# One more buffer for finished output blocks, one fewer for exps, in an attention and GeGLU kernel

## The chip, the cores and the metric

The kernel runs on one core of a Trainium2 chip. The metric is device time in microseconds. Times quoted are medians of several executions.

## The reference

Two steps follow each other: an attention with a sliding window over 8 batches of 8 heads (half of the heads plain, half with every fourth position), then a GeGLU block over all 4608 tokens.

```python
scores = scale * q @ k.T;  scores = where(mask, scores, -1e9)
attn = exp(scores - max); attn = attn / sum(attn);  x = attn @ v     # (4608, 512)
g = x @ w_gate;  val = x @ w_val
out = (gelu(g) * val) @ w_out                                        # (4608, 512) float32
```

## The kernel before

The tokens are worked through in 9 chunks of 512. Each chunk has a gate part (the matmuls with `w_gate` and `w_val`, line 808) and an output part (the matmuls with `w_out`, line 842). The attention of the batches that later chunks need is woven in between: scores on TensorE, their exponentials on ScalarE (the exps, line 693), then the masking, a product with the mask on VectorE (line 698). TensorE sums up in accumulator banks; an eviction is the copy of a finished bank into an output block in SBUF, the on-chip memory (line 853). The parts that matter here, cut:

```python
prb = ctx.enter_context(tc.tile_pool(name="prb", bufs=7))     # exps
osbp = ctx.enter_context(tc.tile_pool(name="osbp", bufs=3))   # finished output blocks
# ...
def two_p_of(n):                       # exp of head pair n
    pt = prb.tile([P, LP], F16, tag="P", name=f"P{n}")
    nc.scalar.activation(pt[:, 0 : src.shape[1]], src, AF.Exp, bias=0.0, scale=scale)
# ...
def store(c, tb, bank, eng):           # block tb of chunk c: empty the bank, send it away
    osb = osbp.tile([P, DM], F32, tag="osb")
    if eng == "act":
        nc.scalar.activation(osb, ps[:, bank, :], AF.Copy, bias=0.0, scale=1.0 / USCALE)   # line 853
    # ...
    nc.sync.dma_start(out=out[t0 : t0 + P, :], in_=osb)                                    # line 857
```

The order of the program is the order by hand. A word like `e3@2` in it means "store block 3 of chunk 2", a number means "so many matmuls", and `R` stands for `load_rest(3)`, `load_first(4)`, `load_rest(4)`, that is, for the loads of two batches, all of them issued from SyncE (`nc.sync`):

```python
gates = {
    2: "G 6 e3@1 R 2 g0 3 u0 ...",     # chunk 2, gate part: the last store of chunk 1, then R
    3: "G 6 e3@2 2 g0 3 u0 2 g1 ...",  # chunk 3, gate part: the last store of chunk 2
}
```

So the fourth store of a chunk runs at the start of the next chunk, and the stores of chunk 2 stand behind `R` in SyncE's queue.

The softmax here doesn't subtract the row's maximum and nothing guards it: scores larger than these inputs give would overflow.

## Time and profile before

| | |
|---|---|
| time | 353.54 us (3 runs, 351.2 to 355.06) when the prediction was made |
| the profiled execution | 357.36 us, span 355.2 us |
| TensorE busy | 336.1 us, 95% of the span |
| VectorE, ScalarE, GpSimd | 175.6, 148.4 and 131.8 us |
| mean granted TensorE clock | 0.986 |

TensorE is the bound nearly everywhere.

### The profile page before, as it was taken

Reading aid. Unit: us, or ns where it says so; the run is one execution under the profiler, and the core shown is the slowest. Engines: PE = TensorE matmul, PEld = TensorE weight load, DVE = VectorE, ACT = ScalarE, POOL = GpSimd, SP = SyncE. Lnnn points to the kernel's source line nnn. Section 1 sums busy time; section 2 is a strip of 40 time slices with the busy share of each in tenths; the row PEclk is TensorE's granted clock in tenths of the full one; section 3 lists DMA queues with packets and bytes.
Section 4 is the critical chain, followed back from the end, with each engine's and each line's share of the span. In section 5 each row is a group of like instructions: output and inputs, shape, how many; then the busy total and the mean of one; then the engine's idle time right before and its main releaser. Section 6 shows DMA issues by size and latency. Waiting matters only on the chain.

```text
span 355.2 us, 5961 instructions
## 1 busy us (share of the span) xinstructions
PE 336.1 (95%) x2264; PEld 168.3 (47%) x2264; DVE 175.6 (49%) x276; ACT 148.4 (42%) x219; POOL 131.8 (37%) x193
## 2 busy tenths in 40 slices
PE   8889999599999999399999999999999999999996
PEld 3644454244554455144555456445654444444443
DVE  3786687244354444134598349744983204403320
ACT  2753372243683367134543357335533243322321
POOL 8892414498503738836604660376000000000000
PEclk9999999699999999899999999999999999999999
DMA  8999997998219779899449943894100020011002
GB/s 179 221 203 218 201 199 169 277 210 193 89 56 191 180 196 186 220 225 189 155 111 215 179 120 103 219 203 128 62 30 2 30 89 2 1 67 53 0 30 89
DMA packets 107804, 48.74 MB, mean 137 GB/s; under 512 B 84481, under 2 KB 103297, under 8 KB 107777
## 3 DMA queue, kind: packets, MB, share of 16 engines
q1 hardware_dynamic: 98208, 41.24, 50.2%
q0 software_dynamic: 9024, 6.43, 11.9%
q10 hardware_dynamic: 544, 0.72, 0.8%
q8 instruction: 17, 0.28, 0.3%
q14 instruction: 11, 0.08, 0.1%
HBM read 38.27 MB, written 9.44 MB: 134 GB/s over the span
## 4 chain that ended last, share of the span: by engine, by line
PE 65%; DMA 15%; SPq 9%; POOL 4%; DVE 4%; issue 2%; ACT 0%; POOLq 0%; DVEq 0%; ACTq 0%
PE ps L808 41%; PE ps L842 18%; DMA wo<-in_moe_w_out_dram 6%; PE ps L752 3%; DMA stage<-in_v_dram 3%; SPq L286 3%; DMA dense<-s 2%; DMA out_dram<-osb 2%; SPq L220 2%; PE ps L678 2%; SPq L289 2%; SPq L323 1%; DMA stage<-in_q_dram 1%; POOL q L346 1%; DVE xT L800 1%
## 5 line engine op out<-in xcount | busy, mean ns | idle before, releaser
L808 PE MATMUL ps<-xT,wv 128*128 128x512 f16 x432 | 115.8, 385 | 9.3 <-ACT osb L853 9.3
L1022 DVE SCALAR_TENSOR_TENSOR u_all<-g,ps 128x512 f16<-128x512 f16 x96 | 65.9, 686 | 112.8 <-PE ps L808 94.5
L808 PE MATMUL ps<-xT,wg 128*128 128x512 f16 x432 | 116.3, 384 | 1.0 <-POOL xT L934 0.7
L1017 ACT ACTIVATE g<-ps 128x512 f16<-128x512 f32 x96 | 57.2, 597 | 109.1 <-PE ps L808 109.1
L842 PE MATMUL ps<-wo,u_all 128*128 128x512 f16 x420 | 101.1, 379 | 0.1
L808 PEld LDWEIGHTS <-wv 128*128 128x128 f16 x432 | 42.5, 99 | 58.6 <-issue 10.5
L808 PEld LDWEIGHTS <-wg 128*128 128x128 f16 x432 | 42.4, 99 | 54.7 <-issue 7.2
L842 PEld LDWEIGHTS <-u_all 128*128 128x128 f16 x420 | 37.8, 98 | 38.7 <-issue 0.7
L346 POOL COPY q<-dense 64x512 f16<-64x512 f16 (+2 forms) x48 | 30.8, 670 | 28.8 <-DMA dense<-s 27.0
L853 ACT ACTIVATE osb<-ps 128x512 f32<-128x512 f32 x34 | 20.2, 595 | 45.5 <-PE ps L842 28.1
L292 POOL CAST s<-stage 128x1280 f16<-128x1280 f32 x12 | 15.0, 1251 | 47.0 <-DMA stage<-in_q_dram 34.0
L335 POOL CAST v<-stage 64x1152 f16<-64x1152 f32 x24 | 27.6, 1151 | 2.9 <-DMA stage<-in_v_dram 2.0
L693 ACT ACTIVATE P<-ps 128x768 f16<-128x768 f32 (+1 forms) x24 | 20.0, 835 | 18.1 <-PE ps L678 18.0
L800 DVE TENSOR_TENSOR xT<-ps,rb 128x576 f16<-128x576 f32 x24 | 22.4, 932 | 6.0 <-PE ps L752 3.2
L304 POOL CAST s<-stage 128x512 f16<-128x512 f32 x24 | 14.6, 637 | 12.8 <-DMA stage<-in_q_dram 11.1
L770 DVE STREAM_TRANSPOSE dt<-ps 128x576 f32<-128x576 f32 x17 | 13.1, 771 | 10.1 <-PE ps L752 10.1
L752 PEld LDWEIGHTS <-v 128*128 128x128 f16 x240 | 12.3, 98 | 5.6
L830 ACT ACTIVATE g<-ps 128x512 f16<-128x512 f32 x12 | 7.1, 597 | 14.7 <-PE ps L808 14.7
L787 DVE STREAM_TRANSPOSE rb<-rc 128x576 f32<-128x576 f32 x17 | 13.1, 769 | 0.1
L752 PEld LDWEIGHTS <-two_ones 128*128 128x128 f16 x132 | 10.4, 98 | 5.4 <-issue 0.3
L752 PE MATMUL ps<-P,v 128*128 128x96 f16 (+3 forms) x240 | 12.6, 199 | 0.0
L678 PEld LDWEIGHTS <-q 128*128 128x128 f16 x216 | 10.9, 98 | 3.3
(99 smaller groups left out, 231.0 us busy)
## 6 DMA issues: line engine op xcount, KB each, us to landing
out_dram<-osb SPq DMA_DIRECT2D x35, 256.0 KB, 2.1
stage<-in_v_dram SPq DMA_DIRECT2D x34, 128.0 KB, 3.3
stage<-in_v_dram SPq DMA_DIRECT2D x24, 144.0 KB, 4.0
stage<-in_q_dram SPq DMA_DIRECT2D x24, 128.0 KB, 3.2
stage<-in_k_dram SPq DMA_DIRECT2D x24, 128.0 KB, 2.9
stage<-in_q_dram SPq DMA_DIRECT2D x6, 512.0 KB, 4.8
stage<-in_k_dram SPq DMA_DIRECT2D x6, 512.0 KB, 5.7
wo<-in_moe_w_out_dram POOLq DMA_DIRECT2D x3, 512.0 KB, 20.6
```

The lines of the kernel that those rows point to most:

```text
L292: nc.gpsimd.tensor_copy(s16[:, 1280 * t : 1280 * t + 1280].rearrange("p (g k c) -> p k g c", g=2, k=5), st_of(i).rearrange("p (k g c) -> p ...
L335: nc.gpsimd.tensor_copy(dst[half, :, half], st[half])
L346: eng.tensor_copy(dst[half, :, :, half], src[half])
L678: nc.tensor.matmul(psf[:, base + c0 : base + c0 + w], lhs, rhs, start=True, stop=True, skip_group_check=True)
L693: nc.scalar.activation(pt[:, 0 : src.shape[1]], src, AF.Exp, bias=0.0, scale=scale)
L752: nc.tensor.matmul(o, lhs, rhs, start=st, stop=True, skip_group_check=True)
L800: nc.vector.tensor_tensor(dst, num, rb, ALU.mult)
L808: nc.tensor.matmul(ps[:, bank, :], w[:, kc, ns], xT[kc][:, tok], start=first, stop=end)
L842: nc.tensor.matmul(ps[:, bank, :], u_all[:, fc, tb * P : (tb + 1) * P], wo_t[fc // 4][:, fc % 4, :], start=(fc == 0), stop=(fc == NNB - 1),)
L853: nc.scalar.activation(osb, ps[:, bank, :], AF.Copy, bias=0.0, scale=1.0 / USCALE)
L1017: nc.scalar.activation(g, ps[:, gate_banks(c, args[0])[0], :], AF.Gelu)
L1022: nc.vector.scalar_tensor_tensor(u_all[:, nb, :], tiles.pop(("g", nb)), USCALE, val, ALU.mult, ALU.mult)
```

## The change

SBUF is nearly full. A fourth output block (2048 bytes per partition) is wanted so that a block can be filled while older ones still wait for their store, and a buffer for exps (1664 bytes) is given up to make room. Four blocks and seven exps do not fit: the build stops with 8 KB wanted for the blocks and 7.25 KB left.

```diff
-    prb = ctx.enter_context(tc.tile_pool(name="prb", bufs=7))
+    prb = ctx.enter_context(tc.tile_pool(name="prb", bufs=6))
     nrm = ctx.enter_context(tc.tile_pool(name="nrm", bufs=2))
     ffn = ctx.enter_context(tc.tile_pool(name="ffn", bufs=3))
-    osbp = ctx.enter_context(tc.tile_pool(name="osbp", bufs=3))
+    osbp = ctx.enter_context(tc.tile_pool(name="osbp", bufs=4))
```

The instructions on every engine are the same, in the same order.

## The prediction

> **What bounds the kernel now.** I read four views of the kernel before, in this order: the slices of the span, the list of waits, the chain of work that ended last, and the timeline and windows around two places. The slices first (a digit is the busy share of a slice of 8.9 us in tenths; PEclk is the granted TensorE clock in tenths):
>
> ```profile
> PE   8889999599999999399999999999999999999996
> PEclk9999999699999999899999999999999999999999
> ```
>
> TensorE is at 90% or more nearly everywhere after the start, so the kernel is bound by TensorE, except in slices 7 (62 to 71 us, digit 5, clock 6) and 16 (142 to 151 us, digit 3, clock 8). The list of waits (engine and line, what it waited for, us in total, times, longest) says what TensorE waited for there:
>
> ```profile
> ACT osb L853 <- DMA out_dram<-osb: 14.1, 2, 7.2
> PE ps L808 <- ACT osb L853: 9.3, 2, 5.7
> ```
>
> TensorE waited twice, 9.3 us in all, for ScalarE to empty an accumulator bank into an output block (osb). ScalarE itself waited twice, 14.1 us, for the DMA that carries an older output block away: the three blocks were all taken. The other waits of TensorE in that list sum to about 5.5 us, and most lie before 62 us. The timeline, cut to the lines concerned, shows where the DMA came late:
>
> ```profile
> 60.04 0.93 SPq L857 DMA_DIRECT2D out_dram<-osb  x2
> 66.12 0.60 ACT L853 ACTIVATE osb<-ps 128x512 f32<-128x512 f32 x1 [6.87 <-DMA out_dram<-osb]
> 66.77 0.58 PE L808 MATMUL ps<-xT,wv 128*128 128x512 f16 x1 [3.61 <-ACT osb L853]
> ...
> 145.27 1.51 SPq L857 DMA_DIRECT2D out_dram<-osb  x3
> 147.63 0.60 ACT L853 ACTIVATE osb<-ps 128x512 f32<-128x512 f32 x1 [7.22 <-DMA out_dram<-osb]
> 148.28 1.86 PE L808 MATMUL ps<-xT,wv 128*128 128x512 f16 x4 [5.70 <-ACT osb L853]
> ```
>
> The stores are short, but SyncE issues everything in program order. The first store of chunk 0 was ready at 54.2 us (its eviction started at 53.65 and took 0.59) and was issued at 60.04, behind the loads of batch 2. The first store of chunk 2 was ready at 128.8 and issued at 145.27, behind the loads of batches 3 and 4. Each time the fourth block of the same chunk needed exactly that first one's buffer. Its bank is the one that the next chunk's fourth group of matmuls writes, so TensorE stopped.
>
> The stop costs more than its idle time:
>
> ```profile
> 62.20:71.00 8.80, 5.19 (x24) 1.83 (x19) 2.13 (x2) 2.08 (x3) 3.71 (x6) 0.70 1.08 277
> 71.00:142.10 71.10, 71.10 (x483) 36.36 (x482) 31.26 (x46) 37.67 (x55) 40.90 (x64) 0.99 0.75 163
> 142.10:151.00 8.90, 3.20 (x10) 1.11 (x8) 1.37 (x2) 1.57 (x3) 7.22 (x11) 0.81 0.81 220
> ```
>
> These are windows: stretch, length, TensorE busy, weight loads, VectorE, ScalarE, GpSimd, granted clock, DMA share, GB/s. Between the two stops TensorE is busy 71.10 of 71.10 us at clock 0.99. Around them the clock is 0.70 and 0.81: the matmuls after a stop start every 0.43 us instead of every 0.216 us.
>
> **What the Trainium skill says.** "TensorE: Matmul & The Clock Gate", section "What's actually happening": the clock of the array halves after an idle window of about 3.4 us and comes back after about as long a busy time. The trace agrees in kind: stops of 3.61 and 5.70 us, then half rate for 5.8 us and 3.1 us. "DMA: Bandwidth & Descriptors", section "Anatomy of one DMA", says that a wait on a semaphore happens on the issuing sequencer before dispatch. That fits a ready store standing behind a waiting load on SyncE for 16.5 us. "SBUF — State Buffer", section "SBUF: two separate sides", says that a VectorE operation with two SBUF inputs and a GpSimd operation that reads SBUF exclude each other for a whole instruction. The trace agrees: the masking of the exps usually takes 0.49 to 0.59 us, but 1.14, 1.07 and 1.40 us in the three cases that fall on a GpSimd cast. "Perfetto Trace Analysis", section "Optimization Strategy", reads consistent bubbles as a sign of too few buffers. Here there are two lone ones, and the list of waits names the buffer.
>
> **The change part by part.** No instruction is added or removed; only waits move.
>
> Fourth output block. There are 36 output blocks in 9 chunks of 4. With three buffers, block i waits for the store of block i-3; with four, for that of i-4, the same block of the chunk before. Chunk 0 then has no such wait at all. Its fourth eviction can start when its bank is complete, about 61.7 us, and ends at 62.3; the matmul that needs the bank is due at 63.0. The fourth block of chunk 2 needs the store of chunk 1's fourth block, which ScalarE finished at 106.0 and SyncE sent at once, 34 us before it is wanted. Every later block has its older store away in time; the tightest is chunk 3's fourth (wanted at 183 us before, its partner sent at 172 us; after the change about 2 us of slack by my shift below). So both stops go:
> - First stop, idle: starts of matmuls at 62.78 and 66.77 are 3.99 apart instead of 0.22: 3.77 us.
> - First stop, slow clock: 17 matmuls from 66.77 to 73.27 took 6.50 us instead of 17 x 0.216 = 3.67: 2.83 us.
> - Second stop, idle: a group of four started at 141.55, the next matmul at 148.28: 6.73 - 0.86 = 5.87 us.
> - Second stop, slow clock: 8 matmuls from 148.28 to 151.36 took 3.08 instead of 1.73: 1.35 us.
> - Sum: 13.8 us. From 151 us to the end TensorE is busy 200.5 of 204 us (the rest is the tail), so what is won there is kept if the inputs arrive in time.
>
> Six exps instead of seven. Exp n then waits for the last matmul that reads exp n-6. The program makes exps of one chunk in a row and uses nearly all up before the next chunk's. The nearest pair is batch 6's third exp (217.14 us) and the matmuls of batch 5's first (186.99 us): 30 us apart. In the list of waits the exps wait only for their scores, 18.0 us in 19 times, never for a buffer. Cost: 0.
>
> What comes nearer. TensorE gains 6.6 us on the loads of batch 2 and 7.2 us more on those of batches 4 and 5, because SyncE and GpSimd do not get faster there. By the timeline: batch 2's dilated mask is complete on GpSimd at 85.3 us; the first masking ran at 92.86 and moves to 86.3, so 1 us is left. Batch 5's keys are spread at 166.4 us; its first scores ran at 177.7 and move to 170.5 on the same scale, so 4 us are left. Batch 4's values are ready at 149.6, first used after 169: 12 us left. None becomes a wait, if narrowly.
>
> A cost does come. GpSimd's work on batch 5 (164 to 175 us) slides 7.2 us into the stretch from 173 to 190 us, where the chain of work runs through VectorE with hardly any slack. There three or four maskings now fall on GpSimd work. At 0.25 us for the short copies and 0.6 us for the casts (from the excess of 0.55 to 0.9 us of the slowed ones), that is 1.1 us, and about 0.2 us more in chunk 1. I take 1.3 us off: 13.8 - 1.3 = 12.5 us.
>
> **The rivals.**
> 1. The store wait is only replaced: another wait of the same chunk start (gelu table, x of the next batch, mask) holds TensorE. For it: 1 us of slack at batch 2's mask. Against it: the start of chunk 2 (104 us) has the same program and no late store, and TensorE runs through it. If half the gain went, 347 us.
> 2. Loads become the bound after the second stop: SyncE's queue is busy without a break from 107 to 172 us, and the DMA share is near 0.8. If batch 5 came 5 us late, the time would be about 346 us.
> 3. The clock drop is chance: the stop of 3.61 us is barely long enough for it, so unprofiled runs may not always have had it. The runs before spread from 351.2 to 355.06, and the profiled one took 357.36. If the profile overstates the stops by 3.8 us, the gain is 8.7 us and the time 345 us.
> 4. Six exps bite: against it, 30 us of room. It would need a wait of 12 us to cancel the gain.
>
> **Range and chances.** 353.5 - 12.5 = 341.0 us. Everything going through with no collision gives 339.7 us, and the fastest run before suggests 2 us of spread, so the low end is 337.5; rivals 2 and 3 give the high end, 346. Faster by over 2% means under 346.5 us: 0.88. Within 2%: 0.11. Slower by over 2%: 0.01, since nothing is added that works.
>
> **What would show it.** In the profile after, slices 7 and 16 of TensorE should be 9, the clock should nowhere fall below 0.9 after the start, and neither line of the second fence should remain. ScalarE's exps should still wait for scores only. In the stretch after the second stop some maskings should take about 1.1 us, and TensorE should have a few tenths of idle more there. I am wrong if a new wait of several us stands at 63 or 136 us, if scores wait for a load of batch 2 or 5, or if a clock drop stays without a stop before it.

## The result, and the profile after

| | before | after |
|---|---|---|
| first comparison, median | 353.27 us (4 runs) | 342.88 us (4 runs, 342.2 to 343.35) |
| ratio | | 0.9706 (95% interval 0.965 to 0.9763) |
| second comparison, median | 354.32 us (11 runs) | 342.92 us (6 runs, 341.84 to 343.54) |
| ratio | | 0.9688 (0.9652 to 0.9725) |
| span of the profiled execution | 355.2 us | 341.6 us |
| mean granted clock, profiled | 0.986 | 0.995 |

A ratio is the mean time of one kernel's runs over that of the other's of the same rounds, so it is not quite the ratio of the medians. The change makes the kernel faster by about 3%.

The slices of the changed kernel, as in the prediction's first fence:

```profile
PE   8889999999999999999999999999999999999995
PEclk9899999999999999999999999999999999999999
```

Both low digits of TensorE are gone, and the clock is at 9 from slice 2 on. The 8 in slice 1 lies in the first 17 us, before any output block is used; the second trace of the change does not have it.

The windows that answer to the prediction's (stretch, length, then busy TensorE, weight loads, VectorE, ScalarE, GpSimd, clock, DMA share, GB/s):

```profile
62.20:71.00 8.80, 8.80 (x61) 4.20 (x56) 4.85 (x6) 4.61 (x8) 4.75 (x7) 1.00 1.14 262
71.00:142.00 71.00, 70.95 (x484) 36.42 (x483) 32.64 (x46) 37.98 (x57) 47.88 (x73) 1.00 0.82 187
134.00:151.00 17.00, 17.00 (x80) 7.74 (x79) 6.18 (x9) 6.84 (x12) 10.52 (x15) 1.00 0.86 224
```

Where TensorE did 24 matmuls from 62.2 to 71 us it now does 61, busy all the time at full clock.

The timeline of the changed kernel, cut to the evictions of the two blocks concerned, the matmuls that need their banks, and the late store:

```profile
62.04 0.60 ACT L853 ACTIVATE osb<-ps 128x512 f32<-128x512 f32 x1 [2.51 <-PE ps L842]
63.27 0.38 PE L808 MATMUL ps<-xT,wv 128*128 128x512 f16 x1
...
134.40 0.60 ACT L853 ACTIVATE osb<-ps 128x512 f32<-128x512 f32 x1
136.40 1.03 PE L808 MATMUL ps<-xT,wv 128*128 128x512 f16 x4
...
137.18 1.51 SPq L857 DMA_DIRECT2D out_dram<-osb  x3
```

The last line is the instructive one. The stores of chunk 2 are nearly as late as before: the first of them was evicted at 122.6 us and is issued at 137.2, 14.6 us later (16.4 before), behind the loads. But the fourth eviction runs at 134.4, before they are issued, because a fourth buffer is free. The buffer doesn't make the stores earlier; it makes nobody wait for them.

The list of what TensorE waited for in the changed kernel, from its top (us in total, times, longest):

```profile
PE ps L882 <- DVE ones L68: 1.5, 1, 1.5
PE ps L457 <- DMA v<-in_k_dram: 1.1, 1, 1.1
PE ps L808 <- POOL xT L934: 0.7, 2, 0.3
```

No wait for an output block is in it. The exps still wait for their scores alone:

```profile
ACT P L693 <- PE ps L678: 17.9, 19, 1.7
```

One can set the two traces beside each other matmul by matmul, since the order is the same. The gate part of chunk 1 starts at 62.34 us before and at 62.61 after. The 21st matmul of it starts at 73.27 before and at 66.94 after: the first stop was worth 6.33 + 0.27 = 6.60 us. Chunk 3's gate part starts at 139.83 before and 133.81 after, so 6.33 - 6.02 = 0.31 us was lost again in between. Its sixth group of four starts at 151.36 before and 138.12 after: the second stop was worth 13.24 - 6.02 = 7.22 us. At the end the lead is 13.6 us.

### The profile page after: what moved, and what is told of

It is laid out like the page before. It is cut to its first block, busy times and chain, and to the rows that moved or that the text cites. A ratio compares the mean times of both kernels' runs of the same rounds, so it can differ in the third digit from the quotient of the medians.

```text
span 341.6 us, 5964 instructions
## 1 busy us (share of the span) xinstructions
PE 332.9 (97%) x2264; PEld 168.0 (49%) x2264; DVE 176.7 (52%) x276; ACT 148.4 (43%) x219; POOL 133.8 (39%) x193
## 4 chain that ended last, share of the span: by engine, by line
PE 85%; DVE 5%; DMA 3%; POOL 2%; ACT 1%; issue 1%; SPq 1%; POOLq 0%; DVEq 0%
PE ps L808 54%; PE ps L842 23%; PE ps L752 4%; DMA stage<-in_v_dram 3%; PE ps L678 2%; DVE xT L800 1%; DVE dt L770 1%; DVE rb L787 1%; POOL xT L934 1%; PE ps L866 1%; SPq L220 1%; PE ps L601 1%; ACT xT L499 1%; DVE P L698 0%; DVE xT L529 0%
## 5 line engine op out<-in xcount | busy, mean ns | idle before, releaser
L808 PE MATMUL ps<-xT,wg 128*128 128x512 f16 x432 | 114.1, 379 | 0.8 <-POOL xT L934 0.7
L808 PE MATMUL ps<-xT,wv 128*128 128x512 f16 x432 | 113.3, 379 | 0.0
L693 ACT ACTIVATE P<-ps 128x768 f16<-128x768 f32 (+1 forms) x24 | 20.0, 834 | 18.0 <-PE ps L678 17.9
L304 POOL CAST s<-stage 128x512 f16<-128x512 f32 x24 | 15.4, 670 | 9.6 <-DMA stage<-in_q_dram 8.4
```

The costliest lines, as they stand in the source:

```text
L808: nc.tensor.matmul(ps[:, bank, :], w[:, kc, ns], xT[kc][:, tok], start=first, stop=end)
```

## The experiments

All ratios are against the kernel before in the same rounds. The first four runs share 11 runs of it (median 353.79 us), the next four 11 others (354.32 us), the last two again 11 others (354.32 us).

### The exps' half alone

```diff
-prb bufs=7        osbp bufs=3
+prb bufs=6        osbp bufs=3
```

> Six exps, three output blocks (the exps' half of the change alone). My theory: the exps never wait for a buffer (nearest reuse 30 us apart), so the time is that of the kernel before, 353.3 us within 1.5 us, and both stops of TensorE (3.6 us near 63 us, 5.7 us near 142 us) stay. Rival (the smaller number of exps costs something that the fourth output block hides in the change): 354 to 356 us or more, and a wait of the exps on the matmuls that read them.

Measured: 354.97 us, ratio 1.0016 (0.9989 to 1.0043). Both stops stay; its list of waits:

```profile
ACT osb L853 <- DMA out_dram<-osb: 13.7, 2, 7.0
PE ps L808 <- ACT osb L853: 9.0, 2, 5.3
```

Taken by its words the expectation missed: 354.97 us lies outside 353.3 us within 1.5, and inside the rival's 354 to 356. But the kernel before stood at 353.79 us in the same rounds, 1.2 us lower, the interval of the ratio includes 1, and the rival's other sign, a wait of the exps for their readers, is not in the trace. So the exps' half costs nothing that the runs can show (at most 0.4%), and the gain is the fourth block's.

### Three blocks, with one late store issued elsewhere

If the stop comes from a store that stands behind loads on SyncE, issuing that one store from another engine's queue should remove the stop without any buffer.

```diff
-nc.sync.dma_start(out=out[t0 : t0 + P, :], in_=osb)
+(nc.scalar if (c, tb) == (0, 0) else nc.sync).dma_start(out=out[t0 : t0 + P, :], in_=osb)
```

The second run has `(2, 0)` in the place of `(0, 0)`, the third has both.

> Kernel before with its three output blocks, only the store of chunk 0's first block is issued from ScalarE's queue instead of SyncE's. My theory (the store is late because it stands behind loads on SyncE): the first stop goes, the second stays; 6.6 us by the profile (3.77 idle and 2.83 slow clock), some 5 us in the time: 346.7 to 349 us. Rival (three blocks are too few however early the store is issued, since the DMA itself lands late): the stop stays, 353 us.

> Kernel before, only the store of chunk 2's first block is issued from ScalarE's queue. My theory: the second stop goes, the first stays; 7.2 us by the profile (5.87 idle and 1.35 slow clock), 346 to 349 us. Rival (number of blocks as such): 353 us.

> Kernel before with three output blocks and seven exps, the two late stores from ScalarE's queue. My theory: both stops go and the time is that of the change, 342 to 344 us, with no fourth block. Rival: 349 us or more, because a later block now waits in the stead of these.

Measured: chunk 0's store alone 349.57 us, ratio 0.9878 (0.9852 to 0.9904); chunk 2's alone 348.96 us, 0.985 (0.9813 to 0.9888); both 343.59 us, 0.9719 (0.9694 to 0.9744). In the first of them only the second stop is left on TensorE's timeline, and in the second only the first:

```profile
140.18 1.34 PE L808 MATMUL ps<-xT,wv 128*128 128x512 f16 x4 [4.22 <-ACT osb L853]
```

```profile
65.38 0.59 PE L808 MATMUL ps<-xT,wv 128*128 128x512 f16 x1 [2.97 <-ACT osb L853]
```

In the third neither is left, but for 0.3 us. This shows the cause: a store that is held behind loads keeps its output block taken. Three blocks are enough when two of the 36 stores go out early.

The rival of the first expectation, a late landing, has a part in the first stop all the same. In the trace before, chunk 0's first store was issued at 60.04 us and landed 5.7 us later, at 65.70, where the median of the stores is 2.1 us (chunk 2's first took 2.3). The waiting matmul followed 1.07 us after the landing; with a landing after 2.1 us, I estimate from these numbers, it would have started at 63.2 us, where 63.0 was due, and not at 66.77. So the first stop took both, the late issue and the slow landing. The moved store was issued at 57.32 and landed after 3.2 us, at 60.52; no run changes the one without the other.

The single stops are worth 4.2 and 4.8 us; the first time is a little over its expected 346.7 to 349 us. In the first run the store did not go out quite at once: evicted at 53.7 us, it left ScalarE's queue at 57.32, and ScalarE's next evictions stood behind it. In the trace a load of k that counts on the same completion semaphore landed at 57.24; what that means is seen below.

### All stores from ScalarE's queue

The simple form of the same idea: no buffer, no list of exceptions.

```diff
-nc.sync.dma_start(out=out[t0 : t0 + P, :], in_=osb)
+(nc.scalar if eng == "act" else nc.sync).dma_start(out=out[t0 : t0 + P, :], in_=osb)
```

> Three output blocks, seven exps; all stores that ScalarE evicts are issued from ScalarE's queue, so none stands behind a load. My theory: no block is late, both stops go as with the fourth block, but each issue takes some 0.4 us of ScalarE's queue (it took 0.38 us in the last store), and ScalarE is not the bound: 342.5 to 346 us. Rival (stores and loads mixed at once slow the loads, or ScalarE's exps come late): 347 us or more.

Measured: 357.05 us, ratio 1.0076 (1.005 to 1.0102), slower than the kernel before; my expectation was wrong. ScalarE's timeline at the end of chunk 0 (ACTq is its queue):

```profile
53.97 0.59 ACT L853 ACTIVATE osb<-ps 128x512 f32<-128x512 f32 x1
60.47 0.37 ACTq L857 DMA_DIRECT2D out_dram<-osb  x1
60.94 0.60 ACT L853 ACTIVATE osb<-ps 128x512 f32<-128x512 f32 x1 [6.38 <-DMA stage<-in_k_dram]
...
72.95 0.34 ACTq L857 DMA_DIRECT2D out_dram<-osb  x1
73.39 0.60 ACT L853 ACTIVATE osb<-ps 128x512 f32<-128x512 f32 x1 [9.20 <-DMA stage<-in_v_dram]
```

The block is complete at 54.6 us, but its store is issued at 60.47, when a load of k lands that has nothing to do with it. Now ScalarE itself stands still in the meantime, and TensorE waits 2.7 and 7.7 us for it. The wait is not in the kernel's text. The compiled program shows it: the DMAs of SyncE and ScalarE take turns on eight completion semaphores, and each DMA first waits until the one that used its semaphore before it has landed. The waits of this store there, and the DMA that used the semaphore last:

```text
load of k  on SyncE    counts on DMAHW2
store      on ScalarE  waits for DMAHW2 >= 64, and for its own eviction; counts on DMAHW2
```

The trace agrees for all three stores of the timeline that were late: the loads on their semaphores landed at 60.40, 63.12 and 72.87 us, and the stores were issued at 60.47, 63.20 and 72.95. So a store put on another queue still waits for the load that has its turn, and blocks whatever else that queue's engine has to do. Of the two exceptions of the runs before, only chunk 0's store pays for this; chunk 2's store, moved alone, went out at 126.22 us, right after its eviction of 125.59.

### More blocks, fewer exps

```diff
-prb bufs=7        osbp bufs=3
+prb bufs=5        osbp bufs=5        # first run
+prb bufs=4        osbp bufs=4        # second run
```

> Five output blocks and five exps. My theory: four blocks took the last wait for a block off, and five exps still have some 26 us of room, so the time is that of the change: 342 to 344 us. Rival (blocks are still short, hidden elsewhere): 341 us or less. Rival (exps bite): over 345 us.

> Four output blocks, four exps. My theory: batch 5's second exp now waits for the last reader of batch 4's second, which ends about 2 us before it, and others have more room, so at most 1 us is lost: 342.5 to 344.5 us. Rival (every exp given up costs): 346 us or more.

Measured: 343.01 us, ratio 0.9681 (0.9654 to 0.9708), and 342.86 us, ratio 0.9684 (0.9656 to 0.9713). Both are the change's time. A fifth block brings nothing. Four exps cost nothing either. The wait of batch 5's second exp for a reader, which the expectation allowed up to 1 us, is not in the list of waits; the exps' line there is all but the same as with six (17.9):

```profile
ACT P L693 <- PE ps L678: 17.8, 19, 1.7
```

The version with four and four leaves 2 x 1664 bytes per partition of SBUF free against the change, at the same time.

### Unused matmuls in the stops

To price the slow clock apart from the idle time, I filled the stops of the kernel before with matmuls whose results nobody reads. Nothing that waits is touched.

```diff
-1: "16 g0 u0 ..."                    3: "G 6 e3@2 2 g0 3 u0 2 g1 ..."
+1: "3 W12@2 13 g0 u0 ..."            3: "G 6 e3@2 2 g0 3 u0 1 W20@7 1 g1 ..."
+# Wn@b: n times matmul(ps[:, b, :], ones[:, 0:P], ones, start=True, stop=True)
```

> Kernel before with 12 dummy matmuls put ahead of the matmul that waits at the first stop and 20 ahead of the one at the second (32 matmuls, 6.9 us of TensorE time at 0.216 us each, all inside the idle time; results unused). Waits and buffers are untouched. My theory: the clock drop behind the stops is a cost of its own, 4.2 us by the profile of before and some 2 to 4 us in usual runs, so 349.5 to 352 us and a granted clock of 0.995 or more; the waits for the output block stay. Rival (usual runs have no clock drop, the trace of before was an exception, so the idle time is all that counts): 353 to 354 us.

Measured: 351.05 us, ratio 0.9914 (0.989 to 0.9938), and the granted clock is 0.998 to 1.0 in all six runs against 0.984 to 0.99 in the 11 of the kernel before. The second stop in its timeline:

```profile
140.05 4.48 PE L882 MATMUL ps<-ones 128*128 128x512 f16 x20
144.57 1.02 PE L808 MATMUL ps<-xT,wv 128*128 128x512 f16 x4
145.43 1.03 PE L808 MATMUL ps<-xT,wg 128*128 128x512 f16 x4
```

After the fill the groups of four start 0.86 us apart at once, which is the full rate. 32 unused matmuls save 354.32 - 351.05 = 3.3 us: that is the price of the slow clock in usual runs. The version with four and four, of the same rounds, is another 351.05 - 342.86 = 8.2 us faster: that is the price of the stops themselves. Together 11.5 us.

### The kernel before and the change again

> The kernel before once more, for a second trace. My theory (the first trace caught long stops: its execution took 357.4 us against 351 to 355.3 in all others): this trace shows two stops that sum to less than the 13.8 us of the first (idle and slow clock together), by about as much as its time is below 357.4 us. Rival (the stops are the same in every execution and something else was slow in the first one): again 13.8 us within 0.5, at a lower time.

> The change once more with five rounds beside the kernel before. My theory: 342 to 343.5 us, some 11 us below the kernel before (10.4 in the first comparison; 11.5 for five and four exps), so a ratio of 0.968 to 0.971, with neither stop and a granted clock of 0.995 or more. Rival (the gain of 10.4 us was low by chance): 12.5 us or more, ratio under 0.965.

The kernel before, second trace: 355.46 us for the profiled execution, span 353.6. TensorE's timeline at its two stops and behind the second:

```profile
66.87 0.59 PE L808 MATMUL ps<-xT,wv 128*128 128x512 f16 x1 [3.90 <-ACT osb L853]
...
146.88 1.02 PE L808 MATMUL ps<-xT,wv 128*128 128x512 f16 x4 [4.08 <-ACT osb L853]
147.74 1.68 PE L808 MATMUL ps<-xT,wg 128*128 128x512 f16 x4
149.21 1.91 PE L808 MATMUL ps<-xT,wv 128*128 128x512 f16 x4
```

Worked out as in the prediction (idle: distance of starts less the usual distance; slow clock: distance of starts less 0.216 us for each matmul), its stops cost 4.06 + 2.95 + 4.24 + 1.68 = 12.9 us. In the trace of the run with six exps and three blocks, which runs like the kernel before, they cost 3.86 + 2.68 + 5.43 + 1.48 = 13.45 us. So three traces can be compared:

| trace | span, us | stops, us | span less stops, us |
|---|---|---|---|
| before, first | 355.2 | 13.8 | 341.4 |
| six exps, three blocks | 354.6 | 13.45 | 341.15 |
| before, again | 353.6 | 12.9 | 340.7 |
| change, ten executions | 340.1 to 341.6 | 0 | 340.1 to 341.6 |

The stops differ from one execution to the next, and in these three traces a longer span goes with longer stops. The expectation is half met: the stops explain 0.9 of the 1.6 us between the first and the second trace of the kernel before, not all, though the rival's 13.8 us within 0.5 is missed too. What is left without them is the span of the change. The change again: 342.92 us, ratio 0.9688, as the theory had it; TensorE waits for no output block in its trace.

## Why the prediction was right or wrong

**The time.** 341.0 us was predicted with a range of 337.5 to 346, and 342.88 was measured. The direction and the place of the gain were right and its size nearly; the point was 1.9 us too low.

**The fourth block, the sum of 13.8 us.** Right, to the last term, in the trace: 6.60 us for the first stop (predicted 3.77 + 2.83) and 7.22 us for the second (5.87 + 1.35). That a late store behind loads is the cause is shown by the runs with three blocks and one or two stores moved. "The stores are short" was a misreading for the first stop: the line quoted gives the time to issue, and the landing took 5.7 us there. Nor did the stores stand behind waiting loads only: SyncE's list of waits shows 8.3 us of waits in the 16.4 us before chunk 2's store, and none in the 5.8 us before chunk 0's, which went on issuing loads. TensorE's other waits sum to 5.9 us, not 5.5; nothing hangs on it.

**From the trace to the time.** Here lies the miss. The step was "353.5 - 12.5 = 341.0 us": it takes the stops of one execution off the median of others. The profiled execution was the slowest of all, 357.36 us, and it was so partly because its stops were long. Taken off its own time, 357.36 - 13.8 = 343.6 us, the sum meets the 343.35 us of the profiled execution after. Rival 3 of the prediction named this effect, and it is what was seen in a weaker form: it put the gain at 8.7 us, and the gain is 10.4 us in the first comparison and 11.4 us in the second. Its suspicion that unprofiled runs sometimes lack the clock drop is right in part. In the first trace the clock is at half for 6.83 us around the first stop (65.72 to 72.55 us) and for 3.41 us around the second (147.64 to 151.05), three pieces of 3.41 us in all. Each such piece takes about 0.005 off the mean clock, so I estimate the pieces of the other executions of the kernel before from their clocks: of 37 executions with a clock, 17 have three (0.984 to 0.986, mean time 354.9 us), 18 have two (0.988 to 0.99, 353.7 us) and two have one (0.995, 352.1 us). So each has some of the drop, the profiled one as much as any, and filling the stops brings 3.3 us.

Luck helped the point: without the 1.3 us taken off for contention, which did not show, it would have been 339.7 us, 3.2 too low.

**Six exps.** The predicted cost of 0 holds; six with three blocks are no slower than seven, and four are enough.

**What comes nearer.** Neither batch 2's mask nor batch 5's keys became a wait. Chunk 3's fourth block found its buffer free: the store it needed landed at 165.6 us, 4.3 us before its eviction (predicted 2).

**The contention of VectorE and GpSimd, 1.3 us.** The collisions are there, but that the change adds any is not shown. In the trace after, nine maskings take over 0.7 us, where three did before; in the second traces of the two kernels it is five in each. Three of them on VectorE's timeline, and from GpSimd's (POOL) the cast that the third falls on:

```profile
91.70 0.85 DVE L698 TENSOR_TENSOR P<-P,high 128x832 f16<-128x832 f16 x1
126.84 0.91 DVE L698 TENSOR_TENSOR P<-P,high 128x832 f16<-128x832 f16 x1
157.29 1.40 DVE L698 TENSOR_TENSOR P<-P,high 128x832 f16<-128x832 f16 x1 [1.80 <-ACT P L693]
...
157.11 1.14 POOL L335 CAST v<-stage 64x1152 f16<-64x1152 f32 x1
```

Five of the nine lie in chunks 1 and 2, not in the stretch after the second stop. TensorE lost 0.31 us up to the start of chunk 3 and won 0.36 us back after the second stop, where in this trace a wait of 0.28 us for VectorE disappeared. The term of 1.3 us measured as about zero net. The expected "few tenths of idle more" for TensorE after the second stop did not come.

**The clock.** "Nowhere below 0.9 after the start" held in the slices.

**A version that beats both.** None of the variants is faster than the change by more than the runs can tell: five and five 343.01, four and four 342.86, the change 342.88 and 342.92 us.

## What to carry to other kernels

When a buffer for finished work runs out, look at when its store is issued as well as at how long it takes: two stores were issued 6 and 16 us late because they stood behind loads in one queue, and one of them then took 5.7 us to land where 2.1 is usual. One more buffer or one store moved remove the same wait; moving every store to a busy engine's queue made that engine wait in the stead. Take a gain that is read from one trace off the time of that same execution, and count the slow clock behind a stop of TensorE as well as the stop.

## What the Trainium skill lacked or had wrong

- "TensorE: Matmul & The Clock Gate", section "What's actually happening": its window of about 3.4 us agrees with the traces, where the clock is at half for 6.83 us, two such windows, at the first stop and for 3.41 us at the second. It says too that the window runs freely; in the second trace of the kernel before the half clock starts at 147.98 us, 1.1 us after the stop of 4.08 us has ended. The page does not tell the remedy that was measured here: unused matmuls in a stop that cannot be avoided saved 3.3 us of 354.3.
- "DMA: Bandwidth & Descriptors", section "Issuing engines are not separate DMA queues", says that issuing from several engines saves only the time that the sequencer takes to issue, usually little. Here SyncE's queue kept a finished store for 5.8 and for 16.4 us, 8.3 us of the latter in waits, and two of 36 stores issued from a second engine saved 10.2 us.
- I found no page that tells of completion semaphores shared in turn by the queues. Here they held a finished store from 54.6 to 60.5 us, and all stores moved made the kernel slower, 357.05 us against 354.32.
